# Attention and a gated MLP on one core: another order for fifty-two operations of the written-out schedule

## The chip, the core and the metric

The program runs on one core of a Trainium2 chip. The metric is the device time of one launch in microseconds (us). The core's engines each have their own instruction queue and take it strictly in the order in which it was written: PE (TensorE, matrix products and transposes), ACT (ScalarE), DVE (VectorE), POOL (GpSimd) and SP (SyncE, which here only issues DMAs). They wait for each other by semaphores.

## The reference

Four batches, 12 heads, 448 tokens, head dimension 64: causal softmax attention, then the heads side by side (768 columns) go through a gated MLP with a spatial product over the tokens.

```
scores = q @ k.T / 8, masked above the diagonal
attn   = softmax(scores) ;  x = concat_heads(attn @ v)          # (4, 448, 768)
h      = relu(x @ w_in)  ;  u, v = halves of h (512 columns each)
v_n    = (v - mean) / sqrt(var + 1e-6)
v_s    = w_spatial @ v_n + b_spatial                            # over tokens
out    = (u * v_s) @ w_out                                      # (4, 448, 768)
```

## The kernel before, in words

The work goes by pairs of heads: 24 pairs, six for a batch. For a pair `load` (L701) issues four DMAs, two heads of q and two of k, into one of three buffers `qk`. For pairs 0 to 9 PE turns q and k with a matmul against the identity (`qk_turn`, L738 for pair 0, head by head, and L764 for the others), ACT or DVE copies the result out of a PSUM bank, and PE makes the scores in fp32 (`wide`, L934), four banks and then a last product; DVE adds the mask and finds the row's extreme (L972), ACT takes the exponent (L982), one of three engines scales by the inverse sum (L487, L489, L491), PE turns the weights back (L1021) and multiplies by v (L1255). Later pairs split q and k into two fp16 parts and are turned by DMA (L828, L1229, products L1101 and L1102). After six pairs `ffn` does the batch's MLP, whose products all have line L1473. Beside the first pairs the weights are made ready: `prep_in` loads `w_in` (L1324), and `gram` (L583) and `total` (L604) find scales.

The order is written by hand as numbers. Every `plan.add` makes one operation with a number; the table `ORDER` holds all 2,496 numbers, and `Plan.run` goes through it once. Each operation is put at the end of its engine's queue, so the order on an engine is the order in the table. Buffers of a kind (`qk`, `ps`, `e`, ...) are handed out in the table's order too, the one freed first going to the next that asks.

`Plan.run` does one more thing. It keeps a planned time for every engine, from costs that stand in the code and from the operations of the table met so far. Where a PE operation's planned start lies later than PE's planned end, it puts filling matmuls between (L689: 128x256 fp16 of ones into PSUM buffer `pf2`, which nobody reads), as many as fit, until planned time 46,000 ns or the first use of `pf2`:

```
if busy[e] < WARM and (2, []) in free["pf"]:
    now = max([busy[e], 2700] + ...)
    while now + (fill := FILL if now > 6000 else 2 * FILL) < start - 40:
        order.append((self.warm, e))
        now += fill
```

A rule of that plan lets no POOL operation start before the DVE operations marked `lock` that stand earlier in the table, and the other way round (`pool_end`, `dve_end`). So a planned start hangs on how the engines' operations lie between each other in the table, even where the order on each engine is the same. The plan only places the fillers; in the program that runs there is no such wait.

Of the kernel before, what the change touches and what calls it, by code (L numbers as in the profile page):

```python
# [56 lines left out]
    10, 1, 5, 0, 3, 73, 8, 6, 72, 100, 2, 75, 74, 4, 9, 14, 12, 11, 15, 96, 13, 26, 97, 22, 98, 93, 7, 16, 148, 18,  # L57
    17, 92, 99, 149, 20, 19, 95, 101, 21, 102, 106, 107, 103, 110, 108, 111, 104, 109, 76, 114, 113, 105, 116, 112,
    115, 27, 120, 118, 117, 157, 28, 119, 94, 121, 164, 126, 132, 160, 158, 165, 127, 122, 161, 166, 78, 23, 167,
    123, 168, 162, 79, 139, 159, 163, 124, 170, 136, 169, 77, 125, 172, 142, 137, 171, 256, 138, 131, 173, 140, 176,  # L60
    29, 152, 141, 143, 177, 257, 153, 30, 190, 128, 193, 150, 174, 133, 178, 24, 154, 151, 130, 129, 144, 175, 156,
    155, 194, 181, 135, 134, 25, 261, 195, 186, 179, 185, 34, 180, 191, 260, 196, 264, 80, 187, 265, 192, 84, 82,
    268, 188, 31, 189, 83, 267, 269, 262, 266, 32, 270, 197, 272, 271, 274, 263, 273, 33, 275, 258, 276, 38, 198,
    182, 81, 35, 259, 46, 278, 36, 184, 277, 315, 279, 280, 37, 183, 316, 318, 285, 42, 282, 253, 283, 284, 319,
    145, 314, 290, 281, 252, 328, 321, 294, 306, 322, 320, 326, 300, 297, 307, 323, 329, 254, 39, 317, 255, 325, 40,
    327, 295, 330, 85, 296, 41, 324, 298, 289, 86, 286, 43, 331, 503, 301, 44, 287, 397, 291, 288, 332, 302, 87, 45,
    202, 310, 88, 334, 402, 47, 333, 311, 89, 500, 338, 90, 336, 335, 146, 206, 351, 398, 48, 293, 147, 344, 348,
    309, 49, 312, 339, 50, 395, 51, 199, 52, 399, 308, 60, 57, 299, 394, 63, 66, 313, 58, 61, 292, 403, 200, 59, 54,
    502, 404, 201, 64, 396, 55, 337, 62, 406, 303, 414, 354, 416, 415, 56, 410, 67, 407, 411, 417, 405, 343, 510,
    409, 207, 412, 572, 208, 501, 413, 509, 203, 587, 69, 422, 423, 507, 418, 573, 304, 439, 588, 419, 204, 408,  # L70
    440, 209, 349, 441, 420, 520, 210, 421, 305, 350, 427, 522, 497, 521, 340, 65, 523, 426, 355, 342, 431, 53, 345,
    341, 356, 352, 424, 205, 400, 70, 428, 425, 346, 524, 68, 214, 401, 589, 347, 498, 353, 429, 506, 496, 430, 525,
    71, 508, 505, 526, 499, 532, 528, 436, 504, 725, 533, 357, 442, 529, 534, 538, 531, 432, 536, 535, 956, 211,
    539, 212, 443, 530, 437, 358, 542, 213, 433, 537, 574, 543, 215, 222, 444, 435, 549, 527, 359, 434, 438, 544,
    216, 734, 511, 91, 545, 540, 513, 445, 561, 737, 548, 541, 738, 558, 512, 741, 217, 739, 562, 546, 742, 554,
    218, 559, 563, 547, 514, 553, 590, 560, 446, 564, 729, 570, 740, 447, 733, 731, 730, 555, 223, 1030, 732, 591,
    557, 743, 224, 728, 550, 556, 744, 726, 565, 225, 552, 515, 727, 566, 551, 735, 1029, 516, 1052, 517, 518, 519,
    955, 567, 751, 219, 907, 745, 977, 747, 746, 752, 220, 748, 736, 908, 1293, 753, 757, 788, 749, 568, 221, 226,
    750, 569, 783, 1292, 785, 754, 795, 784, 770, 791, 592, 781, 796, 786, 762, 755, 227, 792, 779, 763, 593, 756,
    780, 787, 758, 798, 789, 228, 782, 773, 594, 793, 1033, 797, 229, 767, 799, 575, 794, 1031, 230, 800, 231, 771,  # L80
    232, 805, 234, 764, 237, 759, 246, 602, 240, 235, 247, 238, 236, 617, 576, 241, 239, 243, 603, 242, 249, 577,
    806, 244, 362, 801, 363, 817, 604, 248, 360, 595, 766, 760, 361, 802, 364, 765, 618, 365, 761, 807, 250, 790,
    245, 772, 251, 816, 774, 370, 596, 808, 835, 368, 366, 978, 367, 837, 369, 1032, 605, 775, 597, 834, 371, 836,
    811, 606, 812, 833, 838, 818, 373, 824, 813, 598, 819, 820, 768, 599, 372, 803, 607, 769, 839, 600, 374, 814,
    375, 578, 815, 840, 821, 376, 804, 377, 378, 579, 383, 822, 387, 809, 847, 619, 381, 843, 385, 848, 620, 776,
    384, 887, 389, 823, 388, 849, 382, 1051, 850, 386, 841, 777, 810, 580, 390, 844, 641, 827, 888, 778, 825, 601,
    846, 642, 581, 851, 845, 1034, 889, 826, 233, 853, 828, 582, 608, 857, 890, 379, 391, 891, 1053, 583, 852, 893,
    894, 842, 895, 584, 892, 609, 829, 854, 896, 1054, 901, 910, 610, 1058, 1059, 855, 898, 392, 830, 917, 902,
    1055, 393, 856, 611, 903, 448, 899, 460, 913, 585, 612, 858, 911, 1057, 918, 831, 900, 613, 859, 861, 914, 643,
    614, 1060, 921, 644, 586, 904, 919, 862, 860, 832, 615, 655, 920, 616, 621, 915, 622, 864, 449, 876, 656, 869,  # L90
    450, 1291, 623, 877, 1065, 1294, 624, 645, 451, 916, 868, 1290, 646, 625, 879, 452, 870, 1295, 873, 1056, 453,
    626, 657, 1299, 380, 872, 878, 1301, 627, 905, 897, 658, 923, 922, 628, 906, 874, 571, 863, 461, 659, 924, 454,
    629, 462, 1066, 912, 1062, 630, 463, 865, 875, 1067, 484, 871, 660, 866, 1063, 929, 880, 867, 631, 925, 1064,
    980, 632, 927, 661, 992, 926, 633, 930, 634, 1068, 981, 993, 943, 982, 635, 647, 648, 455, 946, 931, 456, 886,
    636, 881, 928, 457, 464, 1004, 994, 939, 983, 1016, 490, 458, 465, 1005, 882, 995, 985, 1061, 1017, 984, 459,
    1069, 932, 996, 997, 986, 1006, 1070, 1018, 987, 998, 485, 637, 999, 1041, 486, 988, 1000, 638, 989, 1300, 487,
    1001, 639, 990, 1306, 466, 1019, 991, 488, 1039, 669, 979, 1007, 909, 1020, 491, 885, 670, 1003, 1021, 489, 944,
    1296, 1002, 933, 671, 1022, 1008, 949, 945, 672, 1010, 1009, 1024, 492, 640, 947, 950, 1011, 934, 493, 662, 948,
    467, 478, 938, 1012, 649, 468, 1013, 940, 1297, 1367, 469, 663, 1015, 883, 472, 470, 1014, 1315, 942, 1303, 951,
    884, 1023, 935, 471, 1304, 1316, 1327, 941, 1307, 1317, 1339, 1305, 937, 673, 494, 664, 1366, 1340, 650, 1308,  # L100
    1298, 1328, 1318, 1368, 1341, 665, 1319, 1369, 1329, 683, 495, 1342, 1370, 666, 684, 1309, 936, 1330, 1320,
    1314, 674, 1321, 1351, 1343, 1332, 1373, 1371, 473, 952, 1331, 1352, 675, 1377, 1322, 1365, 1333, 1374, 1345,
    1344, 1334, 1324, 479, 474, 1380, 685, 480, 1040, 1323, 1353, 1346, 475, 676, 1025, 481, 1335, 677, 1336, 1378,
    678, 1381, 1325, 1038, 1379, 1338, 651, 1348, 1364, 1354, 1337, 1347, 652, 1355, 1326, 953, 1382, 679, 1356,
    954, 653, 1310, 667, 1357, 1383, 1026, 668, 1349, 654, 1350, 958, 1311, 1358, 686, 1027, 680, 482, 1401, 957,
    476, 1028, 1389, 681, 483, 687, 959, 1042, 1413, 960, 961, 964, 682, 962, 1302, 697, 968, 965, 1390, 1414, 698,
    971, 1388, 969, 1415, 708, 1123, 972, 970, 709, 1360, 688, 973, 1425, 1416, 703, 1391, 689, 1035, 974, 699,
    1426, 1417, 704, 477, 966, 1392, 1419, 1418, 1402, 710, 1393, 1124, 1359, 1420, 1403, 700, 1384, 1421, 1394,
    1395, 1422, 711, 701, 1441, 705, 1396, 1424, 1397, 706, 1423, 1440, 1663, 692, 1398, 1439, 975, 693, 976, 1037,
    1664, 963, 1399, 1442, 967, 707, 1400, 1662, 1086, 712, 1098, 1404, 1087, 713, 1044, 694, 1088, 1665, 714, 1099,  # L110
    1089, 1443, 695, 1444, 1438, 1100, 1090, 1140, 1091, 1445, 1447, 1512, 1101, 1451, 1092, 1448, 1093, 715, 1094,
    1385, 1103, 696, 1095, 1452, 716, 1102, 1096, 717, 1453, 1097, 1036, 1104, 1372, 1446, 1110, 1105, 1107, 1454,
    1141, 1111, 1106, 1043, 1142, 1108, 1455, 1112, 1109, 1456, 1406, 1045, 1074, 1405, 1113, 1114, 719, 1075, 1115,
    1073, 1457, 1076, 1046, 1143, 1047, 1077, 1048, 1116, 720, 1078, 1049, 721, 1079, 1119, 1071, 1080, 722, 1081,
# [1646 lines left out]
```

## Time and profile before

| | us |
|---|---|
| median of 3 runs (lowest to highest) | 358.98 (358.64 to 359.28) |
| the profiled execution: its span, first to last instruction | 358.6 |
| busy in it: PE / DVE / ACT / POOL | 346.2 / 285.9 / 268.7 / 161.6 |
| fillers (L689) in it | 32, from 1.5 to 38.0 us |

No device time of its own stands with the profile; its span lies 0.4 under the median of the runs. A matmul's record in the trace is longer than the time that it holds PE, since the next one starts before it ends: two rows of PE overlap where PE goes straight on, and a start is the surer number.

### The profile page before, as it was taken

The numbers are of one execution on the slowest core, as the hardware profiler recorded it, in microseconds if no ns is written. First come the engines' busy times: TensorE is split into PE (matmuls) and PEld (weight loads), VectorE is DVE, ScalarE is ACT, GpSimd is POOL, SyncE is SP. The second block draws the span as 40 slices with busy tenths as digits, with TensorE's granted clock in tenths as the row PEclk, the third lists the DMA queues.
The fourth block names the chain that finished last, engine by engine and source line by source line (L and its number), as shares of the span: only waits on it lengthen the run. The fifth ranks groups of instructions, "written<-read, shape, count | busy, mean of one in ns | idle before, by whom it ended". The sixth has DMA issues, their size and how long they took to land.

```text
span 358.6 us, 8098 instructions
## 1 busy us (share of the span) xinstructions
PE 346.2 (97%) x2602; PEld 225.5 (63%) x2602; DVE 285.9 (80%) x1116; ACT 268.7 (75%) x767; POOL 161.6 (45%) x223
## 2 busy tenths in 40 slices
PE   6999899999999999999999999999999999999995
PEld 5476555665555556765455579755755885555695
DVE  4899889999999999889898998987989994263420
ACT  3698899999999999888799989748789684231101
POOL 3133664337656468364374572334686710042400
PEclk9999999999999999999999999999999999999999
DMA  7959979746768999999997898997767978300014
GB/s 162 210 164 242 244 170 215 174 100 166 150 166 186 208 237 181 178 182 139 188 180 153 172 225 162 205 174 156 164 116 156 159 111 174 82 2 0 3 47 130
DMA packets 160796, 55.84 MB, mean 156 GB/s; under 512 B 155249, under 2 KB 156530, under 8 KB 160754
## 3 DMA queue, kind: packets, MB, share of 16 engines
q1 hardware_dynamic: 160754, 55.33, 74.5%
q8 instruction: 20, 0.33, 0.4%
q14 instruction: 22, 0.18, 0.1%
HBM read 26.76 MB, written 5.51 MB: 90 GB/s over the span
## 4 chain that ended last, share of the span: by engine, by line
PE 65%; DMA 10%; DVE 8%; ACT 7%; POOL 4%; issue 3%; SPq 2%; POOLq 0%; ACTq 0%; DVEq 0%
PE pf L1473 43%; PE px L1255 6%; DMA qkT<-qks 4%; PE ps L1021 3%; PE ps L934 3%; PE ps L1101 3%; ACT e L982 3%; PE ps L1102 2%; DMA et<-e 2%; PE ps L764 2%; POOL qks L523 2%; DVE ps L972 1%; DMA o<-in_moe_w_out_dram 1%; DMA wst<-wb 1%; ACT e L489 1%
## 5 line engine op out<-in xcount | busy, mean ns | idle before, releaser
L1473 PE MATMUL pf<-wi,xT 128*128 128x512 f16 (+1 forms) x360 | 61.6, 338 | 0.0
L1473 PE MATMUL pf<-xT,wi 128*128 128x448 f16 x288 | 59.3, 353 | 0.4 <-ACT hv L1536 0.4
L1124 ACT ACTIVATE ps<-ps,sm 128x384 f32<-128x384 f32 (+4 forms) x98 | 45.4, 463 | 13.2 <-DVE sm L1112 8.0
L1473 PE MATMUL pf<-wo,g 128*128 128x384 f32 x288 | 54.9, 341 | 0.0
L1213 DVE SCALAR_TENSOR_TENSOR e<-ps,sm,e 128x256 f16<-128x256 f32 (+4 forms) x98 | 46.3, 505 | 6.3 <-ACT e L489 6.3
L1473 PEld LDWEIGHTS pf<-wo,g 128*128 128x128 f32 x288 | 49.8, 188 | 2.0 <-issue 1.1
L489 ACT ACTIVATE e<-ps,sm 128x256 f16<-128x256 f32 (+4 forms) x98 | 44.3, 509 | 5.5 <-DVE sm L1146 1.9
L1112 DVE CUSTOM_DVE_ANT_0 ps<-ps,mask,sc 128x256 f32<-128x256 f32 (+4 forms) x98 | 47.2, 506 | 1.4 <-PE ps L1102 0.8
L1473 PEld LDWEIGHTS <-wi 128*128 128x128 f16 x288 | 27.4, 98 | 26.7 <-issue 3.0
L1473 PEld LDWEIGHTS <-xT 128*128 128x128 f16 (+1 forms) x360 | 27.2, 103 | 25.4 <-issue 4.7
L491 POOL TENSOR_SCALAR e<-e,sm 128x384 f32<-128x384 f32 (+3 forms) x43 | 23.8, 566 | 41.5 <-ACT e L982 13.6
L982 ACT ACTIVATE e<-ps,sm 128x256 f32<-128x256 f32 (+3 forms) x70 | 34.3, 500 | 4.6 <-DVE sm L972 2.6
L1473 PE MATMUL pf<-wst,vn 128*128 128x448 f16 (+1 forms) x176 | 36.0, 353 | 0.1
L523 POOL TENSOR_TENSOR qks<-qk,qks 112x512 f16<-112x512 f32 x21 | 24.2, 1157 | 20.3 <-ACT qks L489 8.9
L934 PE MATMUL ps<-qkT 64*128 64x128 f32 (+3 forms) x160 | 28.5, 444 | 0.9 <-ACT e L982 0.7
L1102 PE MATMUL ps<-qkT 128*64 128x256 f16 (+4 forms) x196 | 26.3, 284 | 0.4 <-DVE qkT L847 0.4
L1473 PEld LDWEIGHTS <-vn 128*128 128x128 f16 (+1 forms) x176 | 16.8, 98 | 15.2 <-issue 0.5
L1101 PE MATMUL ps<-qkT 128*64 128x256 f16 (+4 forms) x196 | 24.8, 291 | 0.9 <-DVE e L1213 0.7
L972 DVE CUSTOM_DVE_ANT_0 ps<-ps,e 128x128 f32<-128x128 f32 (+2 forms) x60 | 24.3, 441 | 1.2 <-PE ps L934 1.0
L1021 PE MATMUL ps<-ident,e 128*128 128x128 f32 x160 | 23.8, 279 | 1.3 <-POOL e L491 0.5
L1563 POOL TENSOR_TENSOR ln<-ln,mhalf 128x1 f32<-128x1 f32 (+1 forms) x16 | 10.6, 666 | 31.5 <-DVE ln L1555 26.8
L1021 PEld LDWEIGHTS ps<-ident,e 128*128 128x128 f32 x160 | 17.6, 141 | 9.1 <-issue 3.3
(168 smaller groups left out, 729.5 us busy)
## 6 DMA issues: line engine op xcount, KB each, us to landing
wb<-in_moe_w_in_dram SPq DMA_DIRECT2D x12, 512.0 KB, 4.3
vnat<-in_v_dram SPq DMA_DIRECT2D x24, 192.0 KB, 3.9
out_dram<-o SPq DMA_DIRECT2D x12, 384.0 KB, 3.0
qk<-in_k_dram SPq DMA_DIRECT2D x14, 224.0 KB, 4.0
qk<-in_q_dram SPq DMA_DIRECT2D x14, 224.0 KB, 4.2
o<-in_moe_w_out_dram SPq DMA_DIRECT2D x8, 384.0 KB, 4.1
qk<-in_q_dram SPq DMA_DIRECT2D x20, 112.0 KB, 4.8
qk<-in_k_dram SPq DMA_DIRECT2D x20, 112.0 KB, 3.6
```

Source lines behind the costliest of these rows:

```text
L489: nc.scalar.activation(out=dst, in_=src, func=AF.Copy, scale=scale)
L523: lambda e: HANDLE[e].tensor_tensor(out=dst_l(), in0=src(), in1=dst_h(), op=ALU.subtract),
L934: nc.tensor.matmul(out=at(bank)[r0:r0 + rn, o0:o0 + n], lhsT=flat32(t)[rows, q0:q0 + rn], rhs=k32(t)[rows, :n], start=True, stop=True, ski ...
L972: lambda e, ps=ps, n=n, u=u0 + u, sm=sm, o0=o0, h=h: nc.vector.tensor_tensor_reduce(out=at(ps)[:, o0:o0 + n], in0=at(ps)[:, o0:o0 + n], in ...
L982: lambda e, ps=ps, n=n, u=u0 + u, sm=sm, o0=o0, c=c: nc.scalar.activation(out=at(eb)[:, 128 * c:128 * c + n], in_=at(ps)[:, o0:o0 + n], fu ...
L1021: nc.tensor.transpose(out=at(pt)[:, 128 * i:128 * i + 128], in_=e32(at(eb))[:, c0 + i, :], identity=ident)
L1101: nc.tensor.matmul(out=o, lhsT=w, rhs=qkT[:, 2 + x, :n], start=True, stop=False)
L1102: nc.tensor.matmul(out=o, lhsT=w, rhs=qkT[:, 4 + x, :n], start=False, stop=True)
L1112: lambda e, ps=ps, n=n, u=u, sm=sm, o0=o0, m0=m0: nc.vector.tensor_tensor_reduce(out=at(ps)[:, o0:o0 + n], in0=at(ps)[:, o0:o0 + n], in1=m ...
L1124: nc.scalar.activation(out=dst, in_=src, func=AF.Exp, scale=-1.0, bias=at(sm)[:, u:u + 1], accum_out=at(sm)[:, 4 + 2 * u:5 + 2 * u],)
L1213: lambda e, part=part, src=src, sm=sm, u=u: nc.vector.scalar_tensor_tensor(out=part(1), in0=src(), scalar=at(sm)[:, 12 + u:13 + u], in1=pa ...
L1473: nc.tensor.matmul(out=o, lhsT=a(), rhs=rhs, start=(n0 + n == 0), stop=(n0 + n == len(mms) - 1), skip_group_check=len(out_ap()) > 1,)
```

## The change

Only the table `ORDER` differs, with one line more, so that every later line number is one higher (the fillers are L690, the turns L739 and L765, the scores L935, the turns back L1022). The same 2,496 numbers stand in it, 2,281 of them at another place; on the engines themselves few operations change places with a neighbour: five on PE, six on ACT, six on DVE, one on POOL and five DMAs on SP.

```
 ORDER = (
-    10, 1, 5, 0, 3, 73, 8, 6, 72, 100, 2, 75, 74, 4, 9, 14, 12, 11, 15, 96, 13, 26, 97, 22, 98, 93, 7, 16, 148, 18,
+    1, 10, 5, 0, 14, 12, 16, 3, 11, 8, 73, 15, 72, 18, 100, 17, 6, 96, 13, 9, 20, 101, 97, 7, 21, 75, 74, 98, 2,
...
```

PE at the start, before: `qk0` holds pair 0, `qk1` pair 1; the fillers among them are left out where a line of dots stands.

```order
L738 MATMUL ps0_72<-ident_64,qk0_80 64x112 x4
...
L764 MATMUL ps1_73<-ident_64,qk1_81 128x112 x4
...
L764 MATMUL ps2_74<-ident_64,qk1_81 128x112 x4
...
L738 MATMUL ps3_75<-ident_64,qk0_80 64x112 x4
...
L738 MATMUL ps0_72<-ident_64,qk0_80 128x112 x4
...
L738 MATMUL ps3_75<-ident_64,qk0_80 128x112 x4
...
L934 MATMUL ps1_73<-qkT0_84 128x128
L934 MATMUL ps1_73<-qkT0_84 128x256
```

The same place now:

```order
L739 MATMUL ps0_72<-ident_64,qk0_80 64x112 x4
...
L739 MATMUL ps1_73<-ident_64,qk0_80 64x112 x4
L739 MATMUL ps0_72<-ident_64,qk0_80 128x112 x4
...
L765 MATMUL ps2_74<-ident_64,qk1_81 128x112 x4
...
L739 MATMUL ps1_73<-ident_64,qk0_80 128x112 x4
...
L935 MATMUL ps3_75<-qkT0_84 128x128
L935 MATMUL ps3_75<-qkT0_84 128x256
L765 MATMUL ps2_74<-ident_64,qk1_81 128x112 x4
```

Pair 0's turns moved ahead of pair 1's, and pair 0's first score product ahead of pair 1's second turn. From the first turn to the first score product stood 10 fillers and stand 7; one stands behind pair 1's second turn.

SP a little later, before (`qk1` is pair 2's, the last line here loads pair 3's k, 15 DMAs further down in `qk0`):

```order
L876 DMA vnat0_86<-in_v_dram 128x6x64
L876 DMA vnat0_86<-in_v_dram 64x6x64
L876 DMA vnat0_86<-in_v_dram 128x6x64
L1324 DMA wb0_140<-in_moe_w_in_dram 128x1024
...
L701 DMA qk2_82<-in_q_dram 112x4x64 x2
L701 DMA qk0_80<-in_k_dram 112x4x64 x2
```

And now:

```order
L877 DMA vnat0_86<-in_v_dram 128x6x64
L702 DMA qk1_81<-in_k_dram 112x4x64 x2
L877 DMA vnat0_86<-in_v_dram 64x6x64
L877 DMA vnat0_86<-in_v_dram 128x6x64
L1325 DMA wb0_140<-in_moe_w_in_dram 128x1024
```

Pair 3's two loads of k stand 16 DMAs earlier, ahead of the last of v and of `w_in`; pair 3 has the buffer `qk1` instead of `qk0`.

PE in pair 1's scores, before, from the second half of the first four banks' products to the next product:

```order
L934 MATMUL ps0_72<-qkT1_85 128x256
L689 LDWEIGHTS ones_61
L689 MATMUL pf2_79<-ones_61 128x256
L689 LDWEIGHTS ones_61
L689 MATMUL pf2_79<-ones_61 128x256
L689 LDWEIGHTS ones_61
L689 MATMUL pf2_79<-ones_61 128x256
L934 MATMUL ps3_75<-qkT1_85 128x384
```

And now; the dots stand for 18 more pairs of the same two lines:

```order
L935 MATMUL ps0_72<-qkT1_85 128x256
L690 LDWEIGHTS ones_61
L690 MATMUL pf2_79<-ones_61 128x256
...
L690 LDWEIGHTS ones_61
L690 MATMUL pf2_79<-ones_61 128x256
L935 MATMUL ps2_74<-qkT1_85 128x384
```

Three fillers became twenty. In the whole program 32 became 94. Besides this place the new ones stand at four others: pair 2's last weights turned back (the row `L1021 ... 128x128 x4` out of `e1`, and the score product beside it) had 2 fillers and has 15; pair 3's first weights turned back had none and have 10; its second had none (one a little later) and have 20; and pair 3's product with v had none and has 5. These five places have 64 more, the start and two single ones together 2 fewer.

The rest moves by a place or a few: on ACT a copy of pair 0's turn, two sums of squares, an exponent, a scaling and a multiplication; on DVE five operations of later pairs and one of the MLP; on POOL one multiplication.

## Rows read from the trace of the kernel before

**Rows 1.** The page's first part: busy us, share of the span, instructions.
```profile
PE 346.2 (97%) x2602; PEld 225.5 (63%) x2602; DVE 285.9 (80%) x1116; ACT 268.7 (75%) x767; POOL 161.6 (45%) x223
```
**Rows 2.** Windows: length, busy of PE, PEld, DVE, ACT, POOL; clock, DMA, GB/s.
```profile
18.00:20.00 2.00, 2.00 (x17) 1.56 (x16) 1.66 (x6) 2.00 (x7) 1.20 (x3) 1.00 0.01 2
20.00:40.00 20.00, 18.77 (x171) 13.45 (x169) 18.77 (x75) 17.71 (x59) 6.45 (x12) 1.00 0.95 229
40.00:60.00 20.00, 19.46 (x142) 11.37 (x142) 17.34 (x60) 18.22 (x55) 12.59 (x16) 1.00 0.89 201
60.00:320.00 260.00, 256.64 (x2009) 163.98 (x2006) 225.21 (x900) 216.58 (x614) 128.27 (x160) 1.00 0.82 163
```
**Rows 3.** What PE waited for, 0 to 60 us: total, times, longest.
```profile
PE ps L764 <- DMA qk<-in_k_dram: 1.0, 1, 1.0
PE ps L934 <- ACT e L982: 0.7, 1, 0.7
PE ps L1021 <- POOL e L491: 0.5, 1, 0.5
```
**Rows 4.** PE in order of time, 3 to 17 us: start, us, what.
```profile
3.17 0.93 PE L738 MATMUL ps<-ident,qk 112*64 112x112 f32 x4 [1.31 <-DMA qk<-in_q_dram]
3.88 0.85 PE L689 MATMUL pf<-ones 128*128 128x256 f16 x3
4.59 0.98 PE L764 MATMUL ps<-ident,qk 112*128 112x112 f32 x4
5.36 0.85 PE L689 MATMUL pf<-ones 128*128 128x256 f16 x3
...
9.49 0.27 PE L689 MATMUL pf<-ones 128*128 128x256 f16 x1
9.69 2.38 PE L934 MATMUL ps<-qkT 64*128 64x128 f32 x12
...
13.65 0.50 PE L689 MATMUL pf<-ones 128*128 128x256 f16 x3
...
14.96 0.50 PE L689 MATMUL pf<-ones 128*128 128x256 f16 x3
15.40 0.92 PE L934 MATMUL ps<-qkT 64*128 64x384 f32 x4
16.24 0.94 PE L689 MATMUL pf<-ones 128*128 128x256 f16 x7
```
**Rows 5.** PE in order of time, at the other four places.
```profile
24.88 0.99 PE L934 MATMUL ps<-qkT 64*128 64x384 f32 x4
25.85 0.63 PE L1021 MATMUL ps<-ident,e 128*128 128x128 f32 x4
...
32.59 0.92 PE L934 MATMUL ps<-qkT 64*64 64x448 f32 x3
33.44 0.55 PE L1021 MATMUL ps<-ident,e 128*128 128x128 f32 x3
33.82 0.85 PE L583 MATMUL pf<-vnat 128*128 128x128 bf16 x12
34.51 1.26 PE L1021 MATMUL ps<-ident,e 128*128 128x128 f32 x10
...
42.11 1.57 PE L934 MATMUL ps<-qkT 64*128 64x128 f32 x12
43.63 2.04 PE L1255 MATMUL px<-et,vnat 128*64 128x448 f32 x14
```
**Rows 6.** The chain that ended last, in order of time: start, us, what.
```profile
25.48 2.26 ACT e L982 x9
```
**Rows 7.** SP's queue in order of time: start, us, DMAs issued.
```profile
13.90 1.94 SPq L876 DMA_DIRECT2D vnat<-in_v_dram  x3
20.20 0.35 SPq L1324 DMA_DIRECT2D wb<-in_moe_w_in_dram  x1
...
32.68 2.00 SPq L701 DMA_DIRECT2D qk<-in_k_dram  x2
```

253 rows, old and new, of the table ORDER are left out of this document.

## The prediction

> **What bounds the kernel now.** I read the busy shares first: PE is busy in 97% of the span [rows 1]. The windows then say where it is not: of 260 us between 60 and 320 it idles 260.00 - 256.64 = 3.4 us, of 20 to 60 us 1.23 + 0.54 = 1.8 us [rows 2]. PE is the bound over the whole span, with little to give; DVE and ACT follow at 80% and 75%, and in 20 to 60 us they are nearly as full as PE (DVE 36.1, ACT 35.9 of 40 us). Next I asked what PE waits for at the start: one wait of 1.0 us for a load of k, 0.7 us for ACT's exponents, 0.5 us for POOL [rows 3]. Last I read PE in order of time at every place where the order puts more fillers than before [rows 4, 5]: whether the row ahead of the place ends before or after the next row starts tells whether there is a wait to fill. The chain of waits disagrees with PE in one stretch, where it lies on ACT's exponents [rows 6]; that is the seed of the rivals.
>
> **What a filler costs.** Rows of three and of seven fillers give it: 0.94 and 0.50 us for four more, 0.11 us each [rows 4]. [...] A filler waits for nothing, stands in PE's queue, and what stands behind it waits. Where PE has a wait anyway it costs nothing, where PE goes straight on it costs all of its 0.11 us.
>
> **The five places.** They have 64 more, all after the step of the clock: 64 x 0.11 = 7.0 us if nothing covers them. Place by place, the cover:
> 1. Pair 1's second products, 17 more (1.9 us). Three fillers start at 14.96 and the product at 15.40; three take 0.33, so 0.1 us of wait is left [rows 4].
> 2. Pair 2's last weights, 13 more (1.4 us). The row before ends at 24.88 + 0.99 = 25.87, the turn starts at 25.85: no wait [rows 5].
> 3. Pair 3's first weights, 10 more (1.1 us): 32.59 + 0.92 = 33.51 against 33.44, no wait [rows 5].
> 4. Its second, 19 more (2.1 us): 33.82 + 0.85 = 34.67 against 34.51, no wait [rows 5].
> 5. Pair 3's product with v, 5 more (0.55 us): 42.11 + 1.57 = 43.68 against 43.63, no wait [rows 5].
>
> So PE covers 0.1 us of 7.0. Places 2 to 4 hold back turns of the weights, which ACT and DVE copy out and PE multiplies by v: their queues are in order, so they get late too, and have 10% of their time to catch up.
>
> **What comes back.**
> - The wait of 1.0 us for pair 3's k [rows 3]. Two things end it: its two loads now go out where SP stands still, between 15.84 (13.90 + 1.94) and 20.20, with DMA at a share of 0.01 in 18 to 20 us [rows 2, 7], instead of at 32.68; and PE comes there some 5 us later anyway. Behind the moved loads stand two of v and then `w_in`, which waits until 20.20 for its buffer; two issues of about a microsecond (2.00 us for both, [rows 7]) fit into the 4.4 us that SP stands there. I cost the move at nothing for those, -1.0 for PE. What is late next there is the place itself, behind five microseconds of fillers.
> - Pair 0 first. One turn of pair 1 (0.77 us, 4.59 to 5.36) and three fillers (0.71, 3.88 to 4.59) [rows 4] no longer stand ahead of the first score product: it could start 1.5 us earlier, at 8.2. [...] Bounds 0 and -1.5; I take -0.5, nearer to nothing because the turn is only put off by one product.
> - The wait of 0.5 us for POOL, and the 0.1 us at place 1: POOL's scaling hangs on ACT and DVE, which are late too. Bounds 0 and -0.6; I take -0.4.
> - After 60 us PE has 3.4 us of idle time [rows 2]. A late PE goes through a wait without loss where the one it waits for is not late as well. Most are fed by PE; bounds 0 and -3.4, I take -1.0.
> - The single moves on ACT, DVE and POOL are by one to a few places in queues that keep their work; none adds an instruction. Bounds -0.5 and +0.5 by one instruction of ACT (2.26 us for nine records, half of them read-outs, [rows 6]); I take 0.
>
> Sum: 7.0 - 1.0 - 0.5 - 0.4 - 1.0 = +4.1 us. On the profiled execution, 358.6 + 4.1 = 362.7 of span; the median of the runs lies 0.4 above that span, so **363.1 us**. With every bound against the kernel it is 7.0 - 1.0 + 0.5 = +6.5 (365.5), with every bound for it 7.0 - 1.0 - 1.5 - 0.6 - 3.4 - 0.5 = 0 (359.0).
>
> **Rivals.**
> *ACT is the bound at places 2 to 4, and the fillers stand in PE's shadow there.* For it: the chain lies 2.26 us on ACT's exponents at 25.5 us [rows 6]. Against it: PE's rows follow each other there without a hole [rows 5], and an engine that only waits for ACT would show holes. Then places 1 and 5 alone cost 22 x 0.11 = 2.4 us less 1.9 that comes back at the start: +0.5, 359.5 us, no change that can be told. Chance 0.06.
> *Faster: pair 0's early turns and pair 3's early keys are what the start hangs on.* If ACT and DVE, fed 1.5 us earlier by the first score product, set the pace up to 40 us, all fillers fall into PE's waits, and 1.0 + 1.0 us of the returns are left: 357.0 us. It decides if PE, without its new fillers, waited over 0.11 us for each of them, 7 us in the five places; in 20 to 60 us it idles 1.8 [rows 2]. Chance 0.06.
> *The waits that the fillers stand in are real.* The new order may itself hold PE back there, since the table's rule puts fillers only where it plans a wait. The order on the engines speaks against it: almost nothing moves near places 2 to 5. The time would be the same 7.0 us less 2.0 of returns, 364.0; only the cause differs. Chance 0.06.
> [...] Chance 0.05.
> [...]
>
> **How the numbers follow.** The forecast, all five places paid, has 0.77; its own range is 361 to 365.5. The rivals have 0.06, 0.06, 0.06 and 0.05. The range of 360.3 to 365.7 leaves out the case with no change, the faster one and little of the forecast's tails. The measurement tells 0.2% (0.7 us) from no change. Slower by more: 0.77 + 0.06 + 0.05 less a tail of 0.01, 0.87; within: 0.06 and that tail, 0.07; faster: 0.06.
>
> **What would show it.** [...] Pair 3's product with v, at 43.63 us before [rows 5], starts 4 to 6 us later, and the rows ahead of places 2 to 5 run into the fillers, these into the turns, without a hole. The wait for `in_k_dram` is gone. The delay then stays nearly level to the end. Holes of PE around the fillers, or a first score product at 8.2 with the whole start a microsecond earlier and no delay at that product, would make the forecast wrong.

## The result, and the profile after

The changed kernel takes 364.15 us in the median of three executions and 363.83 in six more, against 358.93 and 358.62 us of the kernel before beside them: a ratio of 1.014, interval 1.0115 to 1.0164, and 1.0152, interval 1.0125 to 1.0179. The forecast was 363.1 us, +4.1; measured are +5.2 both times. A fourth execution beside the three, the one with a profile, took 582.84 us at a granted clock of 0.56 and is left out (with it the median is 364.39). The profile shown here is from the repeat (span 362.7 us, its own time 364.55). A second profile of the kernel before was taken too, with a span of 356.5 us and a time of 358.27. The first one's span was 358.6; an execution of the same kernel with that span took 360.36 us, the longest of its 19, so the first profile very likely shows one that took longer than most. That matters below.

A word on names. The text up to here counts some pairs wrongly. By the heads that they load and multiply, the two loads of k that moved, and the wait for k in [rows 3], are pair 4's (heads 8 and 9); the weights at place 2 are pair 1's; the weights at places 3 and 4, and the product with v at place 5, are pair 2's. The places, the rows and the loads themselves are the ones that were meant; below they have their right names, except in the expectations.

The step of the clock, of which the prediction and two expectations speak, is read from the lengths of PE's records alone. In the first profile a single filler's record takes 0.40 to 0.42 us up to 8.67 and 0.27 at 9.49; fillers behind each other stand 0.21 us apart ahead of the step (0.85 us for three, 0.42 for one) and 0.11 behind it, and "half clock" stands for the longer distance. The granted clock is 1.00 on both sides (the third number from the end):

```profile
8.67 0.42 PE L689 MATMUL pf<-ones 128*128 128x256 f16 x1
```

```profile
0.00:5.00 5.00, 2.23 (x11) 1.53 (x12) 2.97 (x17) 1.82 (x2) 3.27 (x21) 1.00 0.50 114
5.00:10.00 5.00, 5.00 (x29) 4.42 (x28) 0.90 (x4) 1.51 (x3) 0.00 (x0) 1.00 0.97 237
10.00:15.00 5.00, 4.33 (x28) 2.09 (x27) 4.51 (x18) 3.22 (x13) 0.00 (x0) 1.00 0.98 201
```

The page's first part, changed kernel, answers to [rows 1]: PE has 5.6 us more work in 62 more matmuls, the others are as busy as they were.

```profile
PE 351.8 (97%) x2664; PEld 231.9 (64%) x2664; DVE 286.4 (79%) x1116; ACT 269.5 (74%) x767; POOL 160.9 (44%) x223
```

PE of the changed kernel in order of time (start, us, what), which answers to [rows 4, 5]. First the start, then the five places:

```profile
3.21 0.93 PE L739 MATMUL ps<-ident,qk 112*64 112x112 f32 x4 [1.36 <-DMA qk<-in_q_dram]
...
8.20 0.42 PE L690 MATMUL pf<-ones 128*128 128x256 f16 x1
8.55 1.23 PE L935 MATMUL ps<-qkT 64*128 64x128 f32 x4
9.71 0.60 PE L765 MATMUL ps<-ident,qk 112*128 112x112 f32 x4
10.15 0.27 PE L690 MATMUL pf<-ones 128*128 128x256 f16 x1
10.35 2.54 PE L935 MATMUL ps<-qkT 64*128 64x128 f32 x12
...
14.61 2.36 PE L690 MATMUL pf<-ones 128*128 128x256 f16 x20
16.89 0.92 PE L935 MATMUL ps<-qkT 64*128 64x384 f32 x4
...
26.09 1.83 PE L935 MATMUL ps<-qkT 64*128 64x384 f32 x8
27.86 1.81 PE L690 MATMUL pf<-ones 128*128 128x256 f16 x15
29.50 0.60 PE L1022 MATMUL ps<-ident,e 128*128 128x128 f32 x4
...
35.90 1.27 PE L690 MATMUL pf<-ones 128*128 128x256 f16 x10
37.00 0.49 PE L1022 MATMUL ps<-ident,e 128*128 128x128 f32 x3
37.33 0.85 PE L584 MATMUL pf<-vnat 128*128 128x128 bf16 x12
38.02 2.35 PE L690 MATMUL pf<-ones 128*128 128x256 f16 x20
40.20 1.58 PE L1022 MATMUL ps<-ident,e 128*128 128x128 f32 x13
...
47.77 0.72 PE L690 MATMUL pf<-ones 128*128 128x256 f16 x5
48.42 2.04 PE L1256 MATMUL px<-et,vnat 128*64 128x448 f32 x14
```

At each place the fillers run into the work behind them: 14.61 + 2.36 = 16.97 against 16.89, 29.67 against 29.50, 37.17 against 37.00, 40.37 against 40.20, 48.49 against 48.42. PE never stood still there, so the work was ready by the time the fillers ended; how much earlier it was ready, these rows alone don't say. Twenty fillers take 2.28 us from the first to the product behind them, 0.11 each. The product with v at place 5, at 43.63 in [rows 5], starts at 48.42.

What is left for the others to do shows in the windows (length, busy of PE, PEld, DVE, ACT, POOL, then the clock, DMA and GB/s), first the second profile of the kernel before, then two of the changed kernel:

```profile
20.00:40.00 20.00, 19.78 (x178) 13.85 (x177) 18.77 (x75) 17.69 (x59) 6.61 (x13) 1.00 1.00 230
```

```profile
20.00:40.00 20.00, 19.94 (x182) 14.78 (x180) 17.37 (x64) 15.20 (x51) 4.63 (x9) 1.00 0.88 210
40.00:60.00 20.00, 19.86 (x162) 13.04 (x159) 15.94 (x60) 17.50 (x47) 13.58 (x17) 1.00 0.70 157
```

In 20 to 40 us PE is now full (19.94; it was at 18.77 in [rows 2], but at 19.78 in the second profile) and ACT has lost 2.5 us of its 17.7. ACT waits for PE: of the time in which it stood idle ahead of its copies of the turned weights, 1.3 us ended on PE's turns before and 5.1 us end on them now, over the whole span:

```profile
L1045 ACT ACTIVATE et<-ps 128x384 f32<-128x384 f32 (+3 forms) x47 | 19.1, 446 | 1.7 <-PE ps L1021 1.3 <-DVE et L1047 0.3
```

```profile
L1046 ACT ACTIVATE et<-ps 128x384 f32<-128x384 f32 (+3 forms) x47 | 19.0, 441 | 5.3 <-PE ps L1022 5.1
```

### The profile page after: what moved, and what is told of

The parts are those of the page before. It is cut to its first block, busy times and chain, and to the rows that moved or that the text cites. A ratio compares the mean times of both kernels' runs of the same rounds, so it can differ in the third digit from the quotient of the medians.

```text
span 580.9 us, 8226 instructions
## 1 busy us (share of the span) xinstructions
PE 574.5 (99%) x2664; PEld 299.7 (52%) x2664; DVE 295.2 (51%) x1116; ACT 277.1 (48%) x767; POOL 160.5 (28%) x223
## 4 chain that ended last, share of the span: by engine, by line
PE 99%; DMA 0%; ACT 0%; issue 0%
PE pf L1474 60%; PE px L1256 11%; PE ps L935 7%; PE ps L1022 5%; PE ps L1102 4%; PE ps L1103 4%; PE pf L690 3%; PE ps L765 2%; PE pf L584 1%; PE ps L739 1%; PE px L605 0%; DMA qk<-in_q_dram 0%; PE pf L605 0%; ACT o L1685 0%
## 5 line engine op out<-in xcount | busy, mean ns | idle before, releaser
L1474 PE MATMUL pf<-wi,xT 128*128 128x512 f16 (+1 forms) x360 | 102.7, 491 | 0.0
L1474 PE MATMUL pf<-xT,wi 128*128 128x448 f16 x288 | 101.6, 532 | 0.0
L1474 PE MATMUL pf<-wo,g 128*128 128x384 f32 x288 | 88.0, 485 | 0.0
L1474 PEld LDWEIGHTS <-wi 128*128 128x128 f16 x288 | 37.4, 133 | 55.6 <-issue 54.9
L1474 PE MATMUL pf<-wst,vn 128*128 128x448 f16 (+1 forms) x176 | 61.6, 531 | 0.0
L1214 DVE SCALAR_TENSOR_TENSOR e<-ps,sm,e 128x384 f16<-128x384 f32 (+4 forms) x98 | 46.2, 504 | 13.1 <-ACT e L490 13.0
L935 PE MATMUL ps<-qkT 64*128 64x128 f32 (+3 forms) x160 | 42.4, 630 | 0.0
L1103 PE MATMUL ps<-qkT 128*64 128x256 f16 (+4 forms) x196 | 38.3, 404 | 0.0
L1022 PE MATMUL ps<-ident,e 128*128 128x128 f32 x160 | 36.6, 386 | 0.0
L1046 ACT ACTIVATE et<-ps 128x384 f32<-128x384 f32 (+3 forms) x47 | 19.3, 426 | 35.9 <-PE ps L1022 34.8
L1256 PE MATMUL px<-et,vs 128*64 128x448 f16 (+3 forms) x336 | 35.8, 376 | 0.0
L1102 PE MATMUL ps<-qkT 128*64 128x256 f16 (+4 forms) x196 | 35.1, 388 | 0.0
```

Of the source, the lines that this page charges most:

```text
L935: nc.tensor.matmul(out=at(bank)[r0:r0 + rn, o0:o0 + n], lhsT=flat32(t)[rows, q0:q0 + rn], rhs=k32(t)[rows, :n], start=True, stop=True, ski ...
L1022: nc.tensor.transpose(out=at(pt)[:, 128 * i:128 * i + 128], in_=e32(at(eb))[:, c0 + i, :], identity=ident)
L1102: nc.tensor.matmul(out=o, lhsT=w, rhs=qkT[:, 2 + x, :n], start=True, stop=False)
L1103: nc.tensor.matmul(out=o, lhsT=w, rhs=qkT[:, 4 + x, :n], start=False, stop=True)
L1214: lambda e, part=part, src=src, sm=sm, u=u: nc.vector.scalar_tensor_tensor(out=part(1), in0=src(), scalar=at(sm)[:, 12 + u:13 + u], in1=pa ...
L1256: nc.tensor.matmul(out=at(px)[64 * h:64 * h + 64, 128 * j:S], lhsT=lhsT, rhs=rhs, start=(j == 0 and t == 0), stop=(j == 3 and t == (0 if t ...
```

## Experiments

All times are medians; the kernel before was run beside each, at 358.6 to 358.8 us. In the kernels with other fillers `Plan.run` takes their number ahead of each PE operation from a table in place of its rule:

```
-WARM, FILL = 46000, 107
+FILLS = {14: 1, 16: 2, 96: 3, ...}
...
+                order += [(self.warm, e)] * FILLS.get(op.n, 0)
```

Line numbers are a few lower in these, with the fillers at L685 or L686.

**The changed kernel again.** No edit.

> The changed kernel as it is, run again for a profile at the full clock and a narrower interval. Both theories: 363 to 365 us. The theory of the paid fillers: PE goes from the fillers into the turns without a hole at all five places, and pair 3's product with v starts 4 to 6 us later than the 43.63 us of before. The theory of the real waits: holes of PE of some us in 13 to 46 us.

Measured: 363.83 us, and no hole at the five places (above). The product with v at place 5 is 4.8 us late against the first profile, as expected, and 6.0 against the second (42.45 there).

**The changed order with 29 fillers.** The table above with `158: 3`, `159: 7`, `137: 1`, `194: 2`, `261: 1`, `263: 2`, `291: 1`, `49: 1` behind the start's eleven.

> The changed order on every engine, with 29 fillers instead of 94: the start's 11 as the change has them, behind them those of the kernel before. Theory of the paid fillers: 65 fewer at 0.11 us are 7.1 us, less the wait or two that open again: 357 to 359 us, at or under the kernel before. Rival, the new order itself holds PE back where the fillers stand: 363 to 364.5 us, with holes of PE in their place.

Measured: 358.00 us, ratio to the kernel before 0.9987 (0.9965 to 1.001). 65 fillers fewer took 5.8 us off; the order alone is no loss, and no gain that can be told. PE in 0 to 60 us waited for (total, times, longest), this kernel:

```profile
...
PE ps L1018 <- POOL e L488: 0.6, 1, 0.6
PE ps L931 <- ACT e L979: 0.3, 1, 0.3
PE ps L761 <- DMA qk<-in_q_dram: 0.3, 1, 0.3
PE ps L1018 <- ACT e L979: 0.2, 1, 0.2
```

Left out are two waits of the start, for the first constants and the first load. With 65 fillers fewer, PE waits 1.4 us behind the start in all, not 7. The rival of the real waits falls.

**The order of before with 94 fillers.** `FILLS` with the changed kernel's numbers in the kernel before.

> The order of before on every engine, with the changed kernel's 94 fillers ahead of the same operations. Theory of the paid fillers: 358.9 + 7.0, less 1.0 for pair 3's keys and up to 1.5 for other waits: 363.4 to 365. Rival, the order costs and the fillers stand in waits: 359 to 360.

Measured: 365.70 us, ratio 1.0207 (1.0176 to 1.0238): +7.1 us for 62 fillers, 0.11 us each and nothing given back. That is past the upper end of the expectation, 365 us. The fillers alone slow the kernel before by more than the change did.

**The start's fillers alone.** The changed order, `FILLS` with the start's eleven.

> The changed order with the start's 11 fillers alone, none behind pair 0's scores. Theory of the paid fillers: at most the 18 of a29 at 0.11 us less, -2 us, and nothing where they stood in waits: 356 to 359, equal to a29 within 1 us, clock full from 10 us on. [...]

Measured: 358.46 us, ratio 0.9999 (0.998 to 1.0018), the same as with 29. So the 18 cost nothing: where they stood PE mostly waits now. PE waits for ACT's exponents 1.0 us twice, against 0.5 us with 29 fillers, and it is busy 1.7 us less in 0 to 60 us (53.9 against 55.6). The granted clock is 1.00 in all four windows from 0 to 320 us.

```profile
PE ps L1018 <- ACT e L979: 1.0, 1, 1.0
PE ps L931 <- ACT e L979: 1.0, 1, 1.0
```

**The kernel before, a second profile.** No edit.

> The kernel before, again, for a second profile of it. If the first profile is a median execution, its delay against the second stays within 0.3 us all along PE and the span is 358.6 us again; if the first was a slow one, as its span plus the 1.9 us that lie around the span in the other runs says (360.5 us against a median of 358.6), PE runs level with it up to a few points and the second ends 1 to 2 us earlier.

Measured: 358.74 us over twelve executions, profile at 356.5 of span and 358.27 of time. PE of this second profile, where [rows 3] have the wait for pair 4's k:

```profile
38.03 0.38 PE L604 MATMUL pf<-wacc,ones 128*128 128x1 f32 x2
38.28 0.58 PE L764 MATMUL ps<-ident,qk 112*128 112x112 f32 x4
38.79 2.10 PE L1255 MATMUL px<-et,vnat 128*64 128x448 f32 x16
```

There is no such wait: the turn follows at 38.28, where the first profile had it at 39.58. Nor do the four profiles of the order of before with other fillers show it. The wait of 1.0 us belonged to one profiled execution of six.

**Places 1 and 2 alone, and places 3 to 5 alone,** in the order of before.

```
+FILLS = {..., 158: 20, ..., 197: 15}              # places 1 and 2, without 263's two
+FILLS = {..., 295: 10, 298: 20, 303: 5}           # places 3 to 5, without 291's one
```

> The order of before with the changed kernel's fillers at places 1 and 2 alone: 30 more. Paid fillers: 30 x 0.11 = 3.3 us, less the 1.0 us wait for pair 3's keys, which stands behind both places: +2.3, 360.9 us. If waits give nothing back: +3.3, 361.9. If ACT hides place 2: +0.9, 359.5.

> The order of before with the changed kernel's fillers at places 3, 4 and 5 alone: 34 more. Paid fillers: 34 x 0.11 = 3.7 us; places 3 and 4 stand ahead of the wait of 1.0 us for pair 3's keys, so +2.7, 361.3 us. If waits give nothing back: +3.7, 362.3. If ACT hides places 3 and 4: +0.5, 359.1.

Measured: 362.24 us (ratio 1.0104, 1.0091 to 1.0117) and 361.78 (1.009, 1.0077 to 1.0103). That is 3.5 us for 30 fillers, as where nothing is given back, and 3.1 for 34, between the two; neither is what ACT's shadow would make. Their sum, 6.6, is near the 7.1 of both together. PE of the kernel with places 3 to 5 shows the price passing on (the fillers, and behind them pair 1's and pair 2's products with v):

```profile
32.48 1.26 PE L685 MATMUL pf<-ones 128*128 128x256 f16 x10
34.60 2.35 PE L685 MATMUL pf<-ones 128*128 128x256 f16 x20
...
40.81 2.10 PE L1251 MATMUL px<-et,vnat 128*64 128x448 f32 x16
44.34 0.72 PE L685 MATMUL pf<-ones 128*128 128x256 f16 x5
44.99 1.24 PE L1251 MATMUL px<-et,vnat 128*64 128x448 f32 x6
```

Ahead of the fillers this execution is 0.8 us earlier than the second profile of the kernel before (pair 1's second products begin at 14.44 against 15.24). At 44.99 it is 2.5 us later (42.45 there): 3.3 us for 34 fillers.

**Pair 4's loads of k put back.** In the changed order with 29 fillers, the two numbers 254 and 255 moved behind 307, and nothing else.

```
-... 76, 94, 78, 254, 255, 79, 77, ...
+... 306, 307, 254, 255, 503, ...
```

> The changed order with 29 fillers, and pair 3's two loads of k put back behind pair 4's loads of q. Theory: the early loads are worth the wait of 1.0 us for the keys, so this is 1.0 us over a29's 358.0, and the wait <- in_k_dram is back in PE's waits. Rival: the loads are hidden either way, or what they hold back costs as much: within 0.4 us of a29.

Measured: 357.85 us against 358.00, ratio to the kernel before 0.9977 (0.9962 to 0.9992). The early loads are worth nothing in the median, and the wait is not back: behind the start PE waits 0.7 us for POOL and 0.2 us for ACT in 0 to 60 us, and for no load. My theory missed here. This interval leaves out 1.0: the new order with few fillers is a little faster here than the kernel before, by 0.3 to 1.4 us, where the 29 and the 11 fillers left that open.

**More fillers at the very start.** `14: 8` for `14: 1`, in the changed order with the other 28 fillers, and in the kernel before with its other 31.

> The changed order with a29's fillers and seven more ahead of the first turn, where PE waits 1.3 us for the first load of q. If the step of the clock follows the time from which PE is busy, it comes up to 1.7 us earlier than in the other runs (6.4 to 9.6 us there) and, with 1.7 us less at half clock, the time falls by up to 0.8 us: 357.0 to 357.6, the first version under the kernel before by more than its noise. Rival, the step comes when it comes: between 6.4 and 9.6 as before, and 357.6 to 358.4, as a29.

> The kernel before with seven more fillers ahead of its first turn and nothing else. If the step of the clock follows PE's first busy time: up to 0.8 us under the kernel before, 357.8 to 358.4. Rival, the step comes when it comes: 358.4 to 359.0.

Measured: 357.52 us (ratio 0.9961, 0.9944 to 0.9977) and 359.38 (1.0016, 1.0 to 1.0032). The first beats both kernels, as expected if the step follows PE's first work. The second is no better than the kernel before and lies above both of its expectations, so an earlier step is not enough in that order. PE at the start, the first and then the second of them:

```profile
1.46 1.89 PE L686 MATMUL pf<-ones 128*128 128x256 f16 x8 [1.46 <-DVE ones L618]
...
5.80 0.55 PE L686 MATMUL pf<-ones 128*128 128x256 f16 x3
...
7.28 0.92 PE L931 MATMUL ps<-qkT 64*128 64x128 f32 x4
```

```profile
3.88 0.66 PE L685 MATMUL pf<-ones 128*128 128x256 f16 x3
4.72 0.57 PE L760 MATMUL ps<-ident,qk 112*128 112x112 f32 x4 [0.17 <-DMA qk<-in_q_dram]
...
8.31 0.57 PE L734 MATMUL ps<-ident,qk 112*128 112x112 f32 x4 [0.73 <-DMA qk<-in_k_dram]
...
8.93 2.38 PE L930 MATMUL ps<-qkT 64*128 64x128 f32 x12
```

Three fillers take 0.55 us of record in the first and 0.66 in the second, against 0.85 ahead of the step and 0.50 behind it [rows 4], and the second's turn at 4.72 takes 0.57 against 0.98. By these lengths the step comes near 5.8 us in the one and between 3.9 and 4.7 in the other; the next earliest are near 6.7 us (a turn of 0.71 us at 6.42 with 29 fillers, one of 0.79 at 6.18 with places 3 to 5, against 0.55). (The windows of the first show a granted clock of 1.00 from 0 us on.) In the order of before PE then runs ahead of pair 0's loads and waits 0.7 us for k, and its first score product starts at 8.93. In the new order pair 0's four loads are among the first six, the first score product starts at 7.28, and no load is waited for. Whether the seven fillers or only the order with few fillers make the 1.3 us, these runs do not settle: the intervals of 0.9961 and of 0.9987 without the seven overlap.

## Why the prediction was right, and which terms were mis-sized

**What a filler costs: right.** 0.11 us, and four experiments with other numbers of fillers lie around it, at 0.09 to 0.12 each: 5.8 us for 65, 7.1 for 62, 3.5 for 30, 3.1 for 34. That the 64 stand behind a step of the clock, as the sum has it, no run shows, since the granted clock is 1.00 from 0 us on; in its place the changed kernel's profile shows fillers 0.21 us apart at 5.85 (0.85 us for three, 0.42 for one) and all those of the five places, from 14.61 on, 0.11 apart.

**The five places have no cover: right.** No hole of PE before or behind the new fillers, at any place, and each half of them costs about its count. The chain on ACT's exponents at 25.5 us [rows 6] was no shadow for PE: when PE got late, ACT waited for PE's turns (5.1 us, above) and got late too. The 0.1 us of wait at place 1 was none: with twenty fillers there it is still left over (2.28 us for 2.2).

**The wait for k, -1.0: wrong.** It was in the profile and not in the kernel: the second profile has no wait there, and putting the loads back costs nothing. The argument took one execution's late load for a property, and gave the term no bounds: it stands whole even in the sum with every bound against the kernel. With it goes the cost of the move on SP, which is nothing, as I had it.

**The base: wrong by its own.** I put 0.4 us around a span of 358.6. In the later profiles time less span is 1.8 to 2.0 us (358.27 and 356.5, 364.55 and 362.7). If that held then too, the profiled execution took about 360.5 us, with a wait of 1.0 us in it that a median one lacks. Added to the median, the sum still came out near, since it is a difference; but the waits that it gave back were partly that execution's.

**Pair 0 first, -0.5: about right, where the step comes alike.** A single filler's record falls from 0.42 us to 0.27 at the step: between 8.20 and 10.15 us in the changed kernel, between 7.89 and 8.84 in the second profile of the kernel before. Ahead of it PE takes about twice as long (fillers 0.21 us apart against 0.11), so twice the time by which the record on the step exceeds a later one gives an estimate of it: near 9.2 us in the one (the product at 8.55, 1.23 us against 0.92) and near 8.8 in the other (a turn at 8.11, 0.90 against 0.55). That later step eats part of the gain in this pair of profiles. Two others both have it behind them by 7.0 us, the changed order with 29 fillers and then the order of before with places 3 to 5; the last line of each is the beginning of pair 1's second products, ahead of which the order of before has the same work and three fillers more:

```profile
6.97 0.27 PE L686 MATMUL pf<-ones 128*128 128x256 f16 x1
...
7.67 0.92 PE L931 MATMUL ps<-qkT 64*128 64x128 f32 x4
...
13.85 0.92 PE L931 MATMUL ps<-qkT 64*128 64x384 f32 x4
```

```profile
6.81 0.27 PE L685 MATMUL pf<-ones 128*128 128x256 f16 x1
...
8.74 2.38 PE L930 MATMUL ps<-qkT 64*128 64x128 f32 x12
...
14.44 0.92 PE L930 MATMUL ps<-qkT 64*128 64x384 f32 x4
```

The first product starts 1.1 us earlier, 7.67 against 8.74. With pair 1's turn now between the products, 0.6 us of it are left at pair 1's second products, 13.85 against 14.44. The wait of 0.7 us for ACT's exponents [rows 3] lies between, and the new order has none there.

**POOL's wait, -0.4: about right.** Behind the start the second profile of before has two waits in 0 to 60 us, the changed one none:

```profile
PE ps L934 <- ACT e L982: 0.7, 1, 0.7
PE ps L1021 <- POOL e L491: 0.7, 1, 0.7
```

ACT's is the one of the start and belongs to the term above. POOL's is back at 0.6 us in the changed order with 29 fillers, so it is the delay by the new fillers that covers it.

**After 60 us, -1.0: wrong.** Nothing came back in the end. Products with v of pairs of the second half, second profile of before and changed kernel, from the chain of waits:

```profile
182.66 1.43 PE px L1255 x24
...
302.90 1.55 PE px L1255 x24
```

```profile
188.85 1.43 PE px L1256 x24
...
308.51 1.55 PE px L1256 x24
```

The delay against the second profile is 6.0 us at the product with v of place 5, 5.3 near 103 us, 6.2 at the first of these, 5.6 at the last and 6.2 in the span. PE's idle time in 60 to 320 us is 3.1 us in the changed kernel's profile, against 3.4 [rows 2], and its waits of 0.2 us and more behind 60 us did not shrink: 2.2 us in the second profile of before, 3.7 in the changed kernel's. They are for ACT and DVE; that these were late because PE, which feeds them, was late fits this, but no run shows it.

Without the 1.0 of the keys and the 1.0 of the later waits the sum is +6.1, and medians say +5.2. So that the forecast of +4.1 came within 1.1 us is in part luck: 2.0 us of its returns did not come, and 0.9 us came back that no term of it holds. The 62 new fillers are 6.8 us of PE; the order with few fillers returns 0.6 by the medians, at the edge of its noise. Why the order returns 1.9 us under 94 fillers (365.70 less 363.83, whose intervals just touch) stays open. In the profile of the 94 in the old order, an execution of 367.23 us and so longer than its median, 2 us of delay come after 100 us, and no run tells why.

Of the rivals, the real waits and ACT's shadow fell by experiments; the faster case would have needed holes that 29 fillers do not leave. The step came near 9.2 us in the changed kernel's profile. In three profiles of the order of before, with the same fillers ahead of it, the same estimate gives 6.7, 8.8 and 9.3 us (turns of 0.79 us at 6.18, 0.90 at 8.11 and 0.77 at 8.88, against 0.55), so the change is not shown to put it off.

## What to carry to other kernels

A rule that fills planned idle time with work spends real time wherever the plan is wrong, and an order that is nearly the same on each engine can make the plan wrong: count the instructions of each engine before and after a reordering, not only their places. On an engine whose rows follow each other without a hole, an added instruction cost its whole issue distance here, 0.11 us, and the delay stayed to the end. Take a wait for a property of the kernel only when two profiles have it.

## What the hardware showed unasked

The step in PE's records, where a single filler's falls from 0.42 us to 0.27, came between 3.9 and 9.3 us in the profiles, and in three of the order of before, with the same fillers ahead of it, at 6.7, 8.8 and 9.3 by the estimate above. Executions of one kernel differ by 3 us (357.2 to 360.0 in twelve of the kernel before); how much of that is the step, no run shows. In the two profiles with seven more matmuls ahead of the first turn it came near 5.8 us and between 3.9 and 4.7.

One execution of the changed kernel had a mean granted clock of 0.71 in its first 20 us and of 0.56 in every stretch behind them, with PE busy for 574.5 of its 580.9 us:

```profile
0.00:20.00 20.00, 17.25 (x81) 10.75 (x83) 10.44 (x50) 9.09 (x28) 5.35 (x25) 0.71 0.80 180
20.00:100.00 80.00, 80.00 (x405) 44.86 (x407) 43.16 (x158) 44.14 (x129) 21.38 (x34) 0.56 0.48 113
```

It did not return in the nine further executions of this kernel, nor in those of the other orders, and its cause is not known.
